# Gating into the final buffer, logits in groups of four, and a column-tiled second expert layer in a fused attention and two-expert-layer kernel

## The chip, the core and the metric

The kernel runs on one core of one Trainium2 chip. TensorE multiplies matrices into PSUM (eight banks of 128 x 512 words), VectorE, ScalarE and GpSimd work on tiles of 128 partitions, and SyncE issues the transfers (DMA). Every engine takes its instructions in the order of the program and waits for others by semaphores. The metric is the time of one execution in microseconds (us); shorter is better. Each verdict compares medians of several executions.

## What is computed

Three stages follow one another on 4608 tokens (8 batches of 576) of 512 features:

```python
# 1. linear attention, 8 heads of 64
q_s = softmax(q, axis=-1);  k_s = softmax(k, axis=2)
kv = einsum('bhsd,bhse->bhde', k_s, v)
x = einsum('bhsd,bhde->bhse', q_s, kv)         # tokens x 512
# 2. first expert layer: w_in 512 x 2048, w_out 2048 x 512
h = x @ w_in
g = h * cos(h)
x = g @ w_out
# 3. second expert layer: 8 experts of 4 slots, w1 512 x 1024, w2 1024 x 512 each
logits = x @ phi                                # 4608 x 32 slots
slot_input = softmax(logits, axis=0).T @ x      # 32 x 512
for e in range(8):
    slot_out[e] = relu(slot_input[e] @ w1[e]) @ w2[e]
out = softmax(logits, axis=1) @ slot_out
```

The kernel never forms `g @ w_out` for all tokens. It multiplies w_out by phi first (the 2048 x 32 matrix `w2sb`), so that logits come straight from g, and it sums g over the tokens with the slot weights before it multiplies by w_out.

## The kernel before

**Parts and tiles.** The tokens are cut into ten parts: parts 0 to 7 of 512 tokens, parts 8 and 9 of 256 (the last 512 tokens in halves). A part has 16 tiles, one for each 128 of the 2048 hidden features; `s = 16*d + f` counts them, and an even part from 2 on and part 8 start at another feature block (`tile_of`).

**A tile of the first expert layer.** `mm1` is 12 matmuls of 128 x 128 by 512 (256 in the halves), because x and w_in are each split into a high and a low word, into one of three PSUM banks `ps_h` (L700). `round_u` (L708 on ScalarE or L710 on VectorE, by the list `V_ACT`), `frac` (L714, VectorE), `sine` (L719) and `square` (L722, ScalarE) and `gate` (L725, VectorE) make g in one of four buffers `T`. `logits` (L736) then takes a pair of tiles: for each tile, one fp32 matmul for each 128 tokens, with the 32 columns of `w2sb` as weights, into 32-partition strips of one bank `ps_LT`: four strips in the wide parts, two in the halves. In the trace an fp32 matmul is two instructions. `g_tr` (L744, VectorE) writes g, transposed in blocks of 32 x 32, into `G`. `G` has 20 rows; a part uses 16 in four quarters, so that a part can begin one quarter of its own while the part before still holds its four. T is given back after logits and transposes.

**After each part.** `p1` copies the logits out, `p2` (L763, L768) spreads them by small matmuls to the partitions where they are needed, `p3` to `p5` make the running maximum and the slot weights, and `g_mm` (L828) multiplies weights and transposed g in 16 tiles of 32 x 32 of the array; `g_add` (L841) adds to the running sum `gacc` with a rescaling. A part's `g_mm` needs all 16 transposes, and the next part's later quarters of G need `g_mm`. For part 9 there is another form (L814): four times the instructions, a quarter of the output, added (L841, narrow) to a sum that `e_fold` has folded to a quarter before (L946, L952).

**The tail.** `e_tr` transposes the folded sum (L965), `e_si` multiplies it by w_out (L976), `e_siT` scales and turns it (L985 to L1000). `e_w1` (L1006) is the first matrix of the second expert layer, for two groups of four experts: weights of 32 columns, four column tiles, 64 instructions a group. `e_h` (L1018, L1020) and `e_hT` (L1028) make the hidden values; `e_w2` (L1040) multiplies by w2 in units of 1 MB, each in 16 tiles of 32 x 32 and four PSUM banks, one for each expert of the group; `e_so` (L1049, L1050) adds the four banks in pairs, `e_sx` (L1058, L1064) spreads the result, and `e_mm` (L1074) with `e_ev` (L1082) and `e_out` (L1085) write nine blocks of 1 MB. The weights, 36 units of 1 MB (`load_unit`, L920), go into buffers as these come free; `units_after` says which operation frees each. `keep_warm` (L1324) puts filler matmuls on TensorE before the first work (37) and in the tail (up to 100).

**The order.** A planner, `Issue`, holds every operation with a cost in us, its predecessors, a ring that it takes a buffer from (`m`: four PSUM banks, `h`: three, `T`: four) and a place. It plays the program through and gives each free engine the ready operation with the lowest place; the order that comes out is the program's order on each engine. Places of repeated operations are read from `PLACES`. The operations of a tile are in `step_ops`, those after a part in `post_ops`, those of the tail at the end. Here the transposes stand behind nearly everything (`TR`), and logits stand 1.6 tiles ahead; in part 0 (`TR0`) both stand ahead:

```python
op(("g", s), DVE, cost(0.06, 0.54), gate, s, at=s, give="h", after=[("sq", s)])
op(("tr", s), DVE, cost(0.08, 0.62), g_tr, s, at=s + tr_at[0], after=[("g", s)] + fresh)
```

`fresh` names the `g_mm` that held this quarter of G.

## Time and profile before

| | |
|---|---|
| median of three executions | 737.7 us (736.66 to 738.56) |
| the profiled execution | 738.9 us, of which the span of the trace is 737.0 us |
| TensorE matmuls busy | 687.9 us, 93% of the span |
| VectorE, ScalarE, GpSimd busy | 559.2, 449.8, 136.1 us |
| mean granted TensorE clock | 0.975 of full |
| transferred | 97.68 MB |

The trace is that of one execution. A row of a timeline gives the start in us from the span's start, the time that the row covers, the engine, the line of the program, the operation, output and input, the shape and how many instructions are merged in it; in brackets stands how long the engine was idle before and what ended that. `PEld` is TensorE loading weights, which overlaps with its matmuls. Matmuls overlap one another too, so the distance between starts says more than the length of a row. In a table by stretch each engine has its busy time and, after the x, its instructions; then come the granted TensorE clock, the share of time in which the 16 DMA engines were busy, and GB/s.

### The profile page before, as it was taken

How to read it: one execution, taken by the hardware profiler on the slowest of the kernel's cores; microseconds unless marked ns; L12 is line 12 of the kernel's file. 1: busy time of each engine (PE TensorE's matmuls, PEld its weight loads, DVE VectorE, ACT ScalarE, POOL GpSimd, SP SyncE). 2: the span in 40 equal slices, each digit the busy share in tenths (PEclk: the TensorE clock that was granted, in tenths of full speed). 3: DMA queues.
4: the chain of work that ended last, by engine and by line, in shares of the span. 5: the costliest groups of instructions: out<-in, count | busy, mean ns of one | idle time of the engine just before them, and what ended most of it. 6: DMA issues, size and time to landing. Idle time of an engine off the chain costs nothing.

```text
span 737.0 us, 17679 instructions
## 1 busy us (share of the span) xinstructions
PE 687.9 (93%) x7516; PEld 499.3 (68%) x7516; DVE 559.2 (76%) x1075; ACT 449.8 (61%) x758; POOL 136.1 (18%) x133
## 2 busy tenths in 40 slices
PE   7688999899999999999999999999999999889991
PEld 7465767677777766776777777677677787754450
DVE  6799999788898888798788887788776878611142
ACT  2669976956867756955947485584565557600041
POOL 3334522321411414114201250021010000000000
PEclk9899999999999999999999999999999999989996
DMA  9989960051241421320151103000030417989748
GB/s 275 335 326 239 330 199 2 1 142 46 60 100 30 117 43 29 81 62 18 30 130 30 29 15 131 2 29 1 2 103 18 163 31 247 374 299 406 309 163 353
DMA packets 69295, 97.68 MB, mean 133 GB/s; under 512 B 40416, under 2 KB 49632, under 8 KB 63968
## 3 DMA queue, kind: packets, MB, share of 16 engines
q1 hardware_dynamic: 69216, 96.55, 39.8%
q8 instruction: 59, 0.97, 0.6%
q14 instruction: 20, 0.16, 0.1%
HBM read 82.90 MB, written 13.63 MB: 131 GB/s over the span
## 4 chain that ended last, share of the span: by engine, by line
PE 70%; DVE 13%; ACT 9%; DMA 3%; issue 3%; POOL 0%; DVEq 0%; ACTq 0%; POOLq 0%
PE ps_h L700 42%; PE ps_m L828 5%; PE ps_LT L736 5%; PE ps_m L1040 2%; PE ps_m L354 2%; PE ps_LT L1324 2%; PE ps_m L493 2%; PE ps_m L395 2%; DVE T L714 2%; ACT T L719 2%; DVE T L725 2%; PE ps_h L1006 2%; ACT T L722 2%; DMA out_dram<-ob 1%; DMA KVB<-in_k_dram 1%
## 5 line engine op out<-in xcount | busy, mean ns | idle before, releaser
L700 PE MATMUL ps_h<-XH,W 128*128 128x512 f32 x1024 | 345.7, 405 | 0.5 <-DVE T L725 0.5
L700 PEld LDWEIGHTS ps_h<-XH,W 128*128 128x128 f32 x1024 | 193.6, 189 | 58.2 <-issue 12.9
L700 PE MATMUL ps_h<-XL,W 128*128 128x512 f32 x512 | 202.4, 395 | 0.7 <-DVE XL L418 0.7
L719 ACT ACTIVATE T<-T 128x512 f32<-128x512 f32 (+1 forms) x160 | 94.3, 589 | 110.9 <-DVE T L714 108.9
L725 DVE SCALAR_TENSOR_TENSOR T<-T,ps_h 128x512 f32<-128x512 f32 (+1 forms) x160 | 100.1, 627 | 46.0 <-ACT T L722 43.9
L700 PEld LDWEIGHTS ps_h<-XL,W 128*128 128x128 f32 x512 | 97.0, 189 | 19.7 <-DVE XL L418 1.2
L714 DVE SCALAR_TENSOR_TENSOR T<-T,ps_h 128x512 f32<-128x512 f32 (+1 forms) x160 | 100.2, 628 | 11.5 <-ACT T L708 9.2
L744 DVE STREAM_TRANSPOSE G<-T 128x512 f32<-128x512 f32 (+1 forms) x160 | 102.0, 648 | 1.6
L722 ACT ACTIVATE T<-T 128x512 f32<-128x512 f32 (+1 forms) x160 | 94.0, 588 | 4.3
L341 POOL TENSOR_TENSOR B<-Q,qm 128x512 f32<-128x512 f32 x34 | 36.4, 1088 | 207.0 <-PE ps_m L354 106.6
L708 ACT ACTIVATE T<-ps_h,magic 128x512 f32<-128x512 f32 (+1 forms) x84 | 53.2, 634 | 32.6 <-PE ps_h L700 32.4
L319 POOL TENSOR_TENSOR Q<-Q,qm 128x512 f32<-128x512 f32 x36 | 38.0, 1066 | 133.7 <-DVE qm L316 132.1
L736 PE MATMUL ps_LT<-T,wphi 128*32 128x128 f32 x1152 | 53.6, 281 | 4.1 <-DVE T L725 3.8
L710 DVE TENSOR_SCALAR T<-ps_h 128x512 f32<-128x512 f32 (+1 forms) x76 | 48.2, 634 | 10.8 <-PE ps_h L700 10.7
L736 PEld LDWEIGHTS ps_LT<-T,wphi 128*32 128x32 f32 x1152 | 29.2, 109 | 33.5 <-issue 18.5
L700 PE MATMUL ps_h<-xe,W 128*128 128x256 f32 x384 | 50.2, 286 | 0.0
L700 PEld LDWEIGHTS ps_h<-xe,W 128*128 128x128 f32 x384 | 46.9, 188 | 3.2 <-issue 3.2
L472 POOL TENSOR_TENSOR KVB<-KVB,km 128x576 f32<-128x576 f32 x28 | 39.2, 1434 | 31.6 <-ACT km L469 31.6
L828 PE MATMUL ps_m<-G,A 32*32 32x512 f32 x1088 | 38.9, 598 | 0.6 <-DVE A L795 0.5
L719 ACT ACT_TABLE_LOAD x29 | 37.2, 1283 | 0.5
L1324 PEld LDWEIGHTS ps_LT<-ones,ident 128*128 128x128 f32 x178 | 27.7, 242 | 10.6 <-issue 8.7
L1324 PE MATMUL ps_LT<-ones,ident 128*128 128x128 f32 x178 | 30.1, 334 | 4.2 <-issue 2.4
(167 smaller groups left out, 771.1 us busy)
## 6 DMA issues: line engine op xcount, KB each, us to landing
w_u<-in_moe_w_dram SPq DMA_DIRECT2D x22, 1024.0 KB, 8.0
KVB<-in_k_dram SPq DMA_DIRECT2D x16, 576.0 KB, 5.1
KVB<-in_v_dram SPq DMA_DIRECT2D x32, 288.0 KB, 6.1
out_dram<-ob SPq DMA_DIRECT2D x9, 1024.0 KB, 10.7
G<-in_moe_w_dram SPq DMA_DIRECT2D x8, 1024.0 KB, 8.4
rwi<-in_moe_w_in_dram SPq DMA_DIRECT2D x7, 1024.0 KB, 9.5
rwo<-in_moe_w_out_dram SPq DMA_DIRECT2D x5, 1024.0 KB, 7.7
wo<-G SPq DMA_DIRECT2D x16, 256.0 KB, 4.9
```

Of the source, the lines that this page charges most:

```text
L472: (nc.vector if dve else nc.gpsimd).tensor_tensor(out=k_t[:, t], in0=k_t[:, t], in1=km[:, t].unsqueeze(1).to_broadcast([128, KC, 64]), op= ...
L700: nc.tensor.matmul(out=u_t[s], lhsT=w[:, wi, kk, o:o + 128], rhs=x[xi][:, kk], start=(kk == 0 and n == 0), stop=(kk == 3 and n == 2),)
L708: nc.scalar.activation(out=t, in_=u_t[s], func=ACTF.Identity, bias=magic)
L710: nc.vector.tensor_scalar(out=t, in0=u_t[s], scalar1=MAGIC, scalar2=None, op0=ALU.add)
L714: nc.vector.scalar_tensor_tensor(out=t, in0=t, scalar=MAGIC, in1=u_t[s], op0=ALU.subtract, op1=ALU.subtract)
L719: nc.scalar.activation(out=t_t[s], in_=t_t[s], func=ACTF.Sin, scale=math.pi)
L722: nc.scalar.activation(out=t_t[s], in_=t_t[s], func=ACTF.Square, scale=math.sqrt(2.0))
L725: nc.vector.scalar_tensor_tensor(out=t_t[s], in0=t_t[s], scalar=1.0, in1=u_t.pop(s), op0=ALU.subtract, op1=ALU.mult)
L736: nc.tensor.matmul(out=lt_t[d][32 * c:32 * c + 32, 0:128], lhsT=w2sb[:, f], rhs=g[:, 128 * c:128 * c + 128], start=(i % NF == 0), stop=(i ...
L744: nc.vector.transpose(out=gs(d)[:, tile_of(d, i)], in_=t_t[s])
L828: nc.tensor.matmul(out=st["gp"][i][32 * c:32 * c + 32].rearrange("p (f b) -> p f b", f=NF), lhsT=ee[o, 32 * j:32 * j + 32], rhs=gs(d)[o, : ...
L1324: nc.tensor.matmul(out=warm[when][:, 0:128], lhsT=ident, rhs=ones, start=True, stop=True)
```

## The change

`gate` writes g straight into its place in `G`, T is given back there, and the transpose is done in place in G after the logits have read it. `logits` takes n tiles at once: in part 0 pairs as before, in parts 1 to 8 fours, in part 9 fours and, at the end, pairs (`NTL`). In the halves, four column tiles hold two tiles at a time, and `p2` sums the two strips. Part 9 uses the common form of `g_mm`; its sum goes to a buffer of its own (`g9`), is folded and is added to the earlier folded sum. `e_w2` uses 128 rows and four column tiles in place of 16 small tiles, into one PSUM bank, and starts after all of `e_w1`; `e_so` and `e_sx` handle the two halves of 256 columns on two engines. The filler is one matmul of 512 columns in fp32r in place of one of 128 in fp32. All places and the lists of who does what are new.

```diff
-    "TR": [352.1, -1.6],
-    "TR0": [-31.4, -260.3],
...
-    "V_ACT": [[2, 3, 5, 7, 9, 10, 11, 13, 15], [0, 1, 2, 4, 8, 10, 13, 14], [1, 5, 6, 8, 9, 11, 12, 14, 15]],
...
+    "TR": [350.5, -1.4],
+    "TR0": [235.9, -125.9],
...
+    "V_ACT": [[0, 4, 5, 8, 9, 10, 11, 12, 13, 14], [2, 3, 4, 5, 6, 7, 8, 9, 10, 11, 13, 14], [0, 3, 6, 7, 8, 10, 11, 14]],
...
+    "NTL": [[1, 3, 5, 7, 9, 11, 13, 15], [3, 7, 11, 15], [3, 7, 11, 13, 15]],
...
-    "TE": [-328.0, -346.1, -469.8, 431.3, -184.9, 140.8],
...
+    "TE": [-84.2, -443.3, -703.4, 431.4, -449.3, 370.8],
...
+    def g_of(s):
+        d, i = divmod(s, NF)
+        return gs(d)[:, tile_of(d, i)]
...
     def gate(s):
         nc.vector.scalar_tensor_tensor(
-            out=t_t[s], in0=t_t[s], scalar=1.0, in1=u_t.pop(s), op0=ALU.subtract, op1=ALU.mult
-        )
...
-    def logits(s):
+            out=g_of(s), in0=t_t.pop(s), scalar=1.0, in1=u_t.pop(s), op0=ALU.subtract,
+            op1=ALU.mult,
+        )
...
+    def logits(s, n):
...
         d = s // NF
-        if s % NF == 1:
+        if s % NF == n - 1:
             lt_t[d] = pst("LT", 1)
-        for i in (s - 1, s):
-            f, g = tile_of(d, i % NF), t_t[i]
-            for c in range(parts[d][2] // 128):
+        k = parts[d][2] // 128
+        m = 4 // k
+        for i in range(s - n + 1, s + 1):
+            f, g, f0 = tile_of(d, i % NF), g_of(i), i % NF
+            for c in range(k):
+                o = 32 * (c + k * (f0 % m))
                 nc.tensor.matmul(
-                    out=lt_t[d][32 * c:32 * c + 32, 0:128], lhsT=w2sb[:, f],
-                    rhs=g[:, 128 * c:128 * c + 128], start=(i % NF == 0), stop=(i % NF == NF - 1),
+                    out=lt_t[d][o:o + 32, 0:128], lhsT=w2sb[:, f],
+                    rhs=g[:, 128 * c:128 * c + 128], start=(f0 < m), stop=(f0 >= NF - m),
                 )
...
     def g_tr(s):
...
-        d, i = divmod(s, NF)
-        nc.vector.transpose(out=gs(d)[:, tile_of(d, i)], in_=t_t[s])
+        nc.vector.transpose(out=g_of(s), in_=g_of(s))
...
-        nc.scalar.copy(out=st["lt"][:r], in_=lt_t.pop(d)[:r, 0:128])
+        nc.scalar.copy(out=st["lt"], in_=lt_t.pop(d)[:, 0:128])
...
     def p2(d, part):
...
         pm = st["r" if part == 0 else "t"] = misc()
         if part == 0:
             for c in range(r // 32):
+                for n in range(c, 4, r // 32):
+                    nc.tensor.matmul(
+                        out=pm[:, 128 * c:128 * c + 128], lhsT=rc[:, n], rhs=st["lt"],
+                        start=(n == c), stop=(n + r // 32 >= 4),
+                    )
+        else:
+            for n in range(0, 128, r):
                 nc.tensor.matmul(
-                    out=pm[:, 128 * c:128 * c + 128], lhsT=rc[:r, c], rhs=st["lt"][:r],
-                    start=True, stop=True,
+                    out=pm[:, 0:r], lhsT=st["lt"], rhs=ident[:, n:n + r], start=(n == 0),
+                    stop=(n + r == 128),
                 )
-        else:
...
     def g_mm(d, jq):
...
-        if d == NB:
-            for j in range(4 * jq, 4 * jq + 4):
-                for i in range(4):
-                    o = slice(32 * i, 32 * i + 32)
-                    for n in range(4):
-                        nc.tensor.matmul(
...
-                            ),
-                            lhsT=ee[o, 32 * j:32 * j + 32],
-                            rhs=gs(d)[o, 4 * n:4 * n + 4, 32 * j:32 * j + 32],
-                            start=(j == 0), stop=(j == 7), tile_position=(32 * i, 32 * n),
-                        )
-            return
...
     def g_add(d, i):
-        nf = NF if d < NB else 4
-        gp = st["gp"][i][:, 0:32 * nf].rearrange("p (f b) -> p f b", f=nf)
-        dst = acc["g"][:, 0:nf, 32 * i:32 * i + 32]
-        if d == 0:
+        gp = st["gp"][i].rearrange("p (f b) -> p f b", f=NF)
+        dst = acc["g"][:, :, 32 * i:32 * i + 32]
+        if d == NB:
+            if i == 0:
+                acc["g9"] = sbt([128, NF, 128], "A", name="g9")
+            dst = acc["g9"][:, :, 32 * i:32 * i + 32]
+            (nc.vector.tensor_copy if i % 2 else nc.scalar.copy)(out=dst, in_=gp)
+        elif d == 0:
             nc.vector.tensor_copy(dst, gp)
         else:
             nc.vector.scalar_tensor_tensor(
...
     def e_fold(part):
...
+        old = acc["g"][:, 0:4].rearrange("p f b -> p (f b)")
+        if part % 2 == 0:
+            src = acc["g9" if part else "g"]
             tl_["fold"] = misc()
             for n in range(4):
...
                     out=tl_["fold"][32 * n:32 * n + 32], lhsT=r32,
-                    rhs=acc["g"][:, 4 * n:4 * n + 4].rearrange("p f b -> p (f b)"),
+                    rhs=src[:, 4 * n:4 * n + 4].rearrange("p f b -> p (f b)"),
...
                 )
+        elif part == 1:
+            nc.scalar.copy(out=old, in_=tl_.pop("fold"))
         else:
-            nc.scalar.copy(
-                out=acc["g"][:, 0:4].rearrange("p f b -> p (f b)"), in_=tl_.pop("fold")
+            nc.vector.scalar_tensor_tensor(
+                out=old, in0=old, scalar=ac, in1=tl_.pop("fold"), op0=ALU.mult, op1=ALU.add
             )
...
     def e_w2(eg, u):
...
-            so_t["p"] = [misc() for j in range(4)]
+            so_t["p"] = misc()
         for q4 in range(4):
-            for j in range(4):
-                o = slice(32 * j, 32 * j + 32)
-                nc.tensor.matmul(
-                    out=so_t["p"][j][32 * q4:32 * q4 + 32], lhsT=tl_["hT"][o, eg, 4 * u + q4],
-                    rhs=ut["w2", eg, u][o, q4], start=(eg == 0 and u == 0),
-                    stop=(eg == 1 and u == 7), tile_position=(32 * j, 32 * q4),
-                )
+            nc.tensor.matmul(
+                out=so_t["p"][32 * q4:32 * q4 + 32], lhsT=tl_["hT"][:, eg, 4 * u + q4],
+                rhs=ut["w2", eg, u][:, q4], start=(eg == 0 and u == 0),
+                stop=(eg == 1 and u == 7),
+            )
...
     def e_so(i):
...
-            so_t["s"] = sbt([128, 2, 512], "gacc", name="so_s")
-        nc.scalar.copy(out=so_t["s"][:, i], in_=so_t["p"][2 * i])
-        nc.vector.tensor_tensor(
-            out=so_t["s"][:, i], in0=so_t["p"][2 * i + 1], in1=so_t["s"][:, i], op=ALU.add
-        )
+            so_t["s"] = sbt([128, 512], "gacc", name="so_s")
+        o = slice(256 * i, 256 * i + 256)
+        (nc.vector.tensor_copy if i else nc.scalar.copy)(out=so_t["s"][:, o], in_=so_t["p"][:, o])
...
-                out=so_t["q"], lhsT=rr.rearrange("p r s -> p (r s)"), rhs=so_t["s"][:, part],
-                start=(part == 0), stop=(part == 1),
+                out=so_t["q"][i][:, 0:256], lhsT=rr.rearrange("p r s -> p (r s)"),
+                rhs=so_t["s"][:, o], start=True, stop=True,
...
-            so_t["b"] = sbt([128, 512], "wphi", name="so")
-            nc.scalar.copy(out=so_t["b"], in_=so_t["q"])
+            if i == 0:
+                so_t["b"] = sbt([128, 512], "wphi", name="so")
+            (nc.vector.tensor_copy if i else nc.scalar.copy)(
+                out=so_t["b"][:, o], in_=so_t["q"][i][:, 0:256]
+            )
...
-           s, act, at=s, take="T", after=[("mm1", s), past("tr", s - 4), past("tl", (s - 4) | 1)])
...
-        op(("g", s), DVE, cost(0.06, 0.54), gate, s, at=s, give="h", after=[("sq", s)])
-        op(("tr", s), DVE, cost(0.08, 0.62), g_tr, s, at=s + tr_at[0], after=[("g", s)] + fresh)
-        if f % 2:
-            op(("tl", s), PE, 0.5 if nt == 512 else 0.4, logits, s, at=s + tr_at[1],
-               after=[("g", s), ("g", s - 1), past("w2_ev", w // 2) if b == 0 else None,
-                      past("p1", d - 1) if f == 1 else None, past("tl", s - 2)]
-               + [past("warm", i) for i in range(NWARM)] * (s == 1))
-            op(("Tfree", s), PE, 0.0, nothing, at=s, give=("T", "T"),
-               after=[("tl", s), ("tr", s), ("tr", s - 1)])
...
+        op(("g", s), DVE, cost(0.06, 0.54), gate, s, at=s, give=("h", "T"), after=[("sq", s)] + fresh)
+        last = [t for t in tls(d) if t >= f][0]
+        if f == last:
+            n = f - max([t for t in tls(d) if t < f] + [-1])
+            op(("tl", s), PE, 0.15 + (0.215 if nt == 512 else 0.11) * n, logits, s, n, at=s + tr_at[1],
+               after=[("g", i) for i in range(s - n + 1, s + 1)]
+               + [past("w2_ev", tile_of(d, i) // 2) for i in range(f - n + 1, f + 1)] * (b == 0)
+               + [past("p1", d - 1) if f == n - 1 else past("tl", s - n)]
+               + [past("tl", i) for i in range(s - n - 3, s)]
+               + [past("warm", i) for i in range(NWARM)] * (d == 0 and f == n - 1))
+            for i in range(s - n + 1, s + 1):
+                op(("tr", i), DVE, cost(0.08, 0.62), g_tr, i, at=i + tr_at[0], after=[("tl", s)])
...
-            op(("g_mm", d, jq), PE, 1.08 if d < NB else 1.6, g_mm, d, jq, at=s0 + po[4], take=None if jq else "m",
+            op(("g_mm", d, jq), PE, 1.08, g_mm, d, jq, at=s0 + po[4], take=None if jq else "m",
...
-            op(("g_add", d, i), DVE, 0.67 if d < NB else 0.25, g_add, d, i, at=s0 + po[5], give="m",
+            on_act = d == NB and i % 2 == 0
+            op(("g_add", d, i), ACT if on_act else DVE, 0.58 if on_act else 0.67, g_add, d, i,
+               at=s0 + po[5], give="m",
...
+               + ([("w2_sum", 7)] if d == 0 else [("p5", d)] + [("g_add", d, 0)] * (i > 0) if d == NB else []))
...
-        nc.tensor.matmul(out=warm[when][:, 0:128], lhsT=ident, rhs=ones, start=True, stop=True)
+        nc.tensor.matmul(
+            out=warm[when], lhsT=ones_r, rhs=ones_r.unsqueeze(1).to_broadcast([128, 4, 128]),
+            start=True, stop=True,
+        )
...
+    op(("fold", 2), PE, 1.0, e_fold, 2, at=L + 24, take="m",
+       after=[("fold", 1)] + [("g_add", D, i) for i in range(4)])
+    op(("fold", 3), DVE, 0.7, e_fold, 3, at=L + 24, give="m", after=[("fold", 2)])
...
-        + [[end[7]], [("tl", L + 15), ("tr", L + 15), ("tr", L + 14)]]
...
+        + [[end[7]], [("g", L + 15)]]
+        + [[("g_mm", D, 1)]] * 2 + [[("fold", 2)]]
...
             op(("w2", eg, u), PE, 0.95, e_w2, eg, u, at=L + TE[4 + eg],
-               take=None if eg or u else "m", n_take=4,
-               after=[("hT", eg), past("w2", eg, u - 1) or past("w2", eg - 1, 7), *lus(("w2", eg, u))])
+               take=None if eg or u else "m",
+               after=[("hT", eg), ("w1", 1, 3, 1), past("w2", eg, u - 1) or past("w2", eg - 1, 7),
+                      *lus(("w2", eg, u))])
...
-        op(("so", i), DVE, 1.2, e_so, i, at=L + 17, give=("m", "m"),
+        eng, a, c = (DVE, 0.36, 0.36) if i else (ACT, 0.33, 0.33)
+        op(("so", i), eng, a, e_so, i, at=L + 17, give=() if i == 0 else "m",
...
-           after=[("sx", 2), ("c3", D), past("om", b - 1), past("oe", b - 2, 3)])
+           after=[("sx", 2), ("sx", 3), ("c3", D), past("om", b - 1), past("oe", b - 2, 3)])
```

## Rows read from the trace of the kernel before

**Rows 1.** The page, its busy line: busy us, share of the span and instructions of each engine.

```profile
PE 687.9 (93%) x7516; PEld 499.3 (68%) x7516; DVE 559.2 (76%) x1075; ACT 449.8 (61%) x758; POOL 136.1 (18%) x133
```

**Rows 2.** The table by stretch, us from the span's start. The stretches are part 5, part 9, the tail up to the last matmul of `e_si`, from there to the end of `e_w2`, and the output.

```profile
387.09:450.11 63.02, 62.59 (x658) 47.10 (x654) 53.08 (x96) 43.30 (x68) 16.89 (x15) 1.00 0.16 48
...
605.71:638.40 32.69, 32.55 (x329) 27.54 (x329) 26.16 (x70) 22.37 (x49) 0.00 (x0) 1.00 0.83 302
638.40:660.42 22.02, 16.28 (x339) 11.43 (x338) 5.90 (x22) 4.72 (x12) 0.00 (x0) 0.85 0.85 314
660.42:703.20 42.78, 41.02 (x703) 20.38 (x704) 6.46 (x6) 1.37 (x2) 0.00 (x0) 1.00 0.80 322
...
707.90:737.00 29.10, 12.04 (x289) 4.60 (x288) 11.42 (x18) 9.64 (x18) 0.00 (x0) 0.79 0.79 326
```

**Rows 3.** Timeline of TensorE's matmuls in part 5, around one pair of logits tiles, and a stretch of the main loop.

```profile
392.43 0.39 PE L700 MATMUL ps_h<-XH,W 128*128 128x512 f32 x1
392.75 0.64 PE L736 MATMUL ps_LT<-T,wphi 128*32 128x128 f32 x16
...
393.67 0.40 PE L700 MATMUL ps_h<-XL,W 128*128 128x512 f32 x1
...
402.33 0.39 PE L700 MATMUL ps_h<-XL,W 128*128 128x512 f32 x1
...
403.01 0.39 PE L700 MATMUL ps_h<-XL,W 128*128 128x512 f32 x1
```

**Rows 4.** Timeline of TensorE's matmuls behind `g_mm`, in part 2 (four logits tiles) and in part 6 (two); each group stands between the last matmul of `g_mm` and the next tile of the main loop.

```profile
209.31 1.08 PE L736 MATMUL ps_LT<-T,wphi 128*32 128x128 f32 x32
210.32 0.49 PE L700 MATMUL ps_h<-XH,W 128*128 128x512 f32 x1
...
471.88 0.64 PE L736 MATMUL ps_LT<-T,wphi 128*32 128x128 f32 x16
472.46 0.50 PE L700 MATMUL ps_h<-XH,W 128*128 128x512 f32 x1
```

**Rows 5.** Timeline of TensorE's matmuls in part 9.

```profile
626.58 4.58 PE L700 MATMUL ps_h<-xe,W 128*128 128x256 f32 x36
631.09 0.63 PE L736 MATMUL ps_LT<-T,wphi 128*32 128x128 f32 x8
631.65 3.14 PE L700 MATMUL ps_h<-xe,W 128*128 128x256 f32 x24
634.71 0.63 PE L736 MATMUL ps_LT<-T,wphi 128*32 128x128 f32 x8
```

**Rows 6.** Who waited for whom: in all, times, the longest (us). The two rows of logits that waited for a gate.

```profile
PEld ps_LT L736 <- DVE T L725: 8.1, 15, 1.5
...
PE ps_LT L736 <- DVE T L725: 3.8, 6, 1.2
```

**Rows 7.** Timeline of VectorE: the gate of the fifth tile of part 6, and the narrow additions of part 9.

```profile
476.48 0.69 DVE L725 SCALAR_TENSOR_TENSOR T<-T,ps_h 128x512 f32<-128x512 f32 x1 [1.36 <-ACT T L722]
...
649.81 1.12 DVE L841 SCALAR_TENSOR_TENSOR gacc<-gacc,ac,ps_m 128x128 f32<-128x128 f32 x4 [3.66 <-PE ps_m L814]
```

**Rows 8.** Timeline of TensorE's matmuls: `g_mm` of part 8 and the fold, then `p2`, `g_mm` of part 9, a group of fillers and the transposes of the tail.

```profile
615.38 2.35 PE L828 MATMUL ps_m<-G,A 32*32 32x512 f32 x64
617.66 0.63 PE L736 MATMUL ps_LT<-T,wphi 128*32 128x128 f32 x8
...
622.92 1.07 PE L946 MATMUL ps_m<-gacc,r 128*32 128x512 f32 x8
...
641.99 0.71 PE L763 MATMUL ps_m<-LTs,rc 64*128 64x128 f32 x4 [0.80 <-ACT LTs L755]
...
644.67 2.45 PE L814 MATMUL ps_m<-G,A 32*32 32x128 f32 x131
648.25 1.87 PE L814 MATMUL ps_m<-G,A 32*32 32x128 f32 x125 [1.13 <-issue]
...
653.07 1.86 PE L1324 MATMUL ps_LT<-ones,ident 128*128 128x128 f32 x7 [2.42 <-issue]
654.73 1.06 PE L965 MATMUL ps_m<-ident,gacc 128*128 128x128 f32 x4
```

**Rows 9.** The chain that ended last, in order of time (start, us, what): `e_w1` of group 0.

```profile
663.76 7.20 PE ps_h L1006 x64
```

**Rows 10.** Timeline of TensorE's matmuls at the end of `e_w2`: two units, fillers, `e_sx`, the first output block.

```profile
699.40 1.14 PE L1040 MATMUL ps_m<-G,hT 32*32 32x512 f32 x32
...
702.00 1.14 PE L1040 MATMUL ps_m<-G,hT 32*32 32x512 f32 x32
703.08 2.05 PE L1324 MATMUL ps_LT<-ones,ident 128*128 128x128 f32 x16
704.96 1.88 PE L1058 MATMUL ps_m<-so_s,rr 128*128 128x512 f32 x4
...
707.89 1.14 PE L1074 MATMUL ps_m<-so,cst 32*32 32x512 f32 x32
```

**Rows 11.** The table by stretch in the second expert layer, before and after the last load has landed.

```profile
684.80:695.50 10.70, 10.30 (x196) 5.76 (x196) 2.71 (x2) 0.69 (x1) 0.00 (x0) 1.00 0.97 402
695.50:703.20 7.70, 7.06 (x149) 3.40 (x138) 0.00 (x0) 0.00 (x0) 0.00 (x0) 1.00 0.03 9
```

**Rows 12.** The table by stretch, 2 us behind the row at 653.07 of rows 8.

```profile
654.00:656.00 2.00, 2.00 (x11) 2.00 (x10) 0.00 (x0) 0.17 (x1) 0.00 (x0) 0.50 0.97 336
```

65 lines of the change are left out of this document (32 added, 33 removed), and 10 rows, old and new, of the table PLACES.

## The prediction, made before the changed kernel was run

> **What bounds the kernel now.** I read the page first, then stretches of the program, then single instructions around the places that the change touches.
>
> The page's busy line [rows 1] names TensorE: 687.9 of 737.0 us, VectorE next with 559.2. The table by stretch [rows 2] says where that holds. In part 5 of the first expert layer TensorE is busy 62.59 of 63.02 us, VectorE 53.08, ScalarE 43.30: what TensorE issues there is the time. The same holds for the last half part (32.55 of 32.69 us), where the DMA share is 0.83 as well. After the last expert-layer tile (638.4) comes a chain with one thing at a time: up to 660.42 VectorE is busy only 5.90 us and TensorE 16.28 of 22.02, much of it filler. From 660.42 to 703.2 the two stages of the second expert layer run, TensorE 41.02 of 42.78 us, DMA share 0.80. From 707.9 the output is written, DMA share 0.79 of 29.1 us; nothing in the change touches its pace, so it only starts earlier or later.
>
> **Logits groups in parts 1 to 7.** A matmul of the main loop follows the one before by 0.227 us (402.33 to 403.01 is three) [rows 3]. Around a lone pair of logits tiles, 392.43 to 393.67 is 1.24 us where two steps would be 0.45: the detour costs 0.79. The pure work of a tile is seen where a group stands behind other small matmuls: four tiles take 1.01 us (209.31 to 210.32), two take 0.58 (471.88 to 472.46) [rows 4], so two tiles are 0.43 and the rest of the 0.79, 0.36 us, is entering and leaving. Groups of four in place of pairs take four groups out of each of the seven parts, 28 in all. If all stood alone: 28 x 0.36 = 10.1 us. If all stood beside other small work: two pairs cost 1.16, one four 1.01, so 28 x 0.15 = 4.2 us. The chain of a part has both kinds, and nothing favours one: I take 7.1 (bounds 4.2 and 10.1).
>
> **Packed columns in the last two half parts.** There a pair of 256-wide tiles keeps two of the four column tiles busy. From 626.58 to 631.09 36 matmuls and an exit take 4.51 us, from 631.65 to 634.71 24 take 3.06, so one is 0.121 us, and 24 of them with the 0.56 of the group and its edges (631.09 to 634.71, 3.62) leave 0.72 for a pair [rows 5]: as much as a pair of twice the width. Eight pairs a part cost 5.8 us. After, part 8 has four groups of four that fill the columns as a 512-wide pair does, 0.79 each, 3.2: a gain of 2.6. Part 9 has three of them and two of two (0.79 less half of 0.43, 0.58): 3.5, a gain of 2.3. Spreading the packed logits back takes two more small matmuls and one more transpose a part; two such take 0.71 in the tail (641.99) [rows 8], so +0.5 in part 8. Together -4.4.
>
> **G in place of T.** A T buffer is given back at the gate, not after logits and transpose. The transpose is the same instruction, now behind the logits group of four. TensorE waited for a gate ahead of logits 8.1 us at weight loads and 3.8 at matmuls, 21 times [rows 6]; 35 of 80 groups go. I count -2.5 (bounds 0 and -5). Some 24 roundings move from VectorE to ScalarE, which has the room [rows 2]. Places, the conversion stage and the warm-up: 0 (bounds -3 and +3), since part 0 keeps its pairs and its loads.
>
> The body: -7.1 - 4.4 - 2.5 = -14.0.
>
> **From the last tile to the expert input.** The wider spreading: +0.5. The last weighted sum goes from 644.67 to 649.81, 256 small instructions with a stall of 1.13 in which TensorE waited for nothing [rows 7, 8]; in the form of the other parts it has 64, which take 2.28 (615.38 to 617.66), twice that at the lower clock: I take 3.2, -1.9 (bounds -2.8 and -0.5). Four narrow adds, 1.12 us together, become four wide copies on two engines, 2 x 0.69 by the wide gate [rows 7]: +0.3. A second fold is new in the chain: 1.07 for its matmuls (622.92), 0.69 for the add, 0.2 for two hand-offs, +2.0. Then between the end of the adds (650.93) and the transposes (654.73) the trace loses 3.8 us to fillers and a stall of 2.42 [rows 8]. It was not waiting for data; a shorter instruction stream should meet less of it, but the new program has fillers too: half, -1.9 (bounds -3.6 and 0). Sum -1.0 (bounds -3.6 and +2.3).
>
> **Second expert layer.** Today its first stage is split by its second: w2 of group 0 runs ahead of most of w1 of group 1, and the last two loads wait for w1 of group 1. The DMA share is 0.97 up to 695.5 and 0.03 after [rows 11], and the last w2 units run at 699.40 and 702.00, with fillers between, ending at 703.08 [rows 10]. After the change all of w1 comes first. A unit in four column tiles is 8 instructions, 0.90 us by the same shape in w1 (7.20 for 64) [rows 9], against 1.07. TensorE's own work from 663.76 is then 14.4 + 16 x 0.90 = 28.8, so 692.6, and the loads set the end: 695.5, 0.5 for landing, 0.9 for a unit, 696.9. That is -6.2; fillers laid ahead of a unit that has landed keep 1.2 of it: -5.0 (bounds -7 and 0).
>
> **Output of the experts.** From 703.08 to 707.89 [rows 10] two copies and two adds run in turn, two wide matmuls (1.88) and a copy. After: a half copy, two half matmuls, a half copy. A half copy is between 0.35 and 0.69 (half and whole of [rows 7]), I take 0.45; the matmuls 0.94; hand-offs 0.3: 2.1, so -2.7, less 0.4 for fillers: -2.3 (bounds -2.8 and -1.0). By the Trainium skill (PSUM — Partial Sum Buffer, PSUM bank collisions raise a hardware error), two engines may not touch one bank and quadrant at a time, so the two half copies of one bank would have to run in turn; by that the estimate is 2.5 in place of 2.1. No run here shows it.
>
> The tail: -1.0 - 5.0 - 2.3 = -8.3.
>
> **The sum.** -14.0 - 8.3 = -22.3 on the profiled execution of 738.9 us (span 737.0 and 1.9 around it): 716.6. The median of the runs shown is 737.7, 1.2 below it, so 715.4.
>
> **Rivals.**
> A, the forecast, 715.4: both halves pay. Chance 0.55.
> B, the body pays, the w2 order does not: fillers and stalls stand where the waits stood, as at 653.07 [rows 8] and 702.00 [rows 10]. Against it: the loads end 7.6 us before the last unit. Then 737.7 - 14.0 - 1.0 - 2.3 = 720.4. Chance 0.18.
> C, TensorE starves while it waits for data in w2. With w1 done early each unit of 0.9 us waits for a load of about 2.6 (34 us for 13 units by the DMA share of that stretch), and TensorE may fall to its lower clock, as it stood at 0.50 of full, 1.2 GHz, at 654 to 656 after idling 2.42 us [rows 8, 12]. The last unit, the half matmuls and the first output block would take twice as long, 0.9 + 0.9 + 1.0: 718.2. Fillers speak against it. Chance 0.12. The Trainium skill (TensorE: Matmul & The Clock Gate, HAM oscillation — how this bites in real kernels) tells of just this: a burst of matmuls shorter than the wait for its load starts at the lower clock each time. The trace at 654 agrees with it.
> D, only the tail pays: the saved detours come back as idle time, because the order of the other engines sets the pace. For it: VectorE is at 84% in part 5. Against it: TensorE at 99%. 737.7 - 8.3 = 729.4. Chance 0.08.
> E, slower: the gate now writes into G, so it, and not the transpose, waits for the weighted sum of the part before. In part 6 that sum's matmuls leave the queue at 471.88 and the gate of the fifth tile starts at 476.48 [rows 4, 7]: 4.6 us in hand. The sum comes later by 0.43 (two more tiles in the last group) and by two more transposes behind it, 1.4: 2.8 us remain. If it came later by more than the 4.6, gate, ps_h and main loop would stop; a stop of 4 us in each of seven parts is 28 us, which outweighs all gains: 737.7 - 22.3 + 28 = 743.4. It decides from 3.2 us a part. Chance 0.05.
> F, no change, since the program's order absorbs it: 737.7, chance 0.02.
>
> **How the numbers follow.** The predicted time is A's. The smallest gain is 4.2 + 4.4 + 0 in the body and -2.3 + 0 + 1.0 in the tail, 7.3 us: 730; with 3 lost at the places 733. The largest is 10.1 + 4.4 + 5 and 3.6 + 7 + 2.8, 32.9: 705; with 3 won at the places 702. All ends at once are unlikely, so 702 to 731 holds A to D with little left out, E and F outside. Faster by over 0.3%, about what a measurement of this kernel can tell from no change (2.2 us): A to D less a little, 0.92; slower 0.05; within 0.03.
>
> **What would show each step.** Parts 1 to 7 shorter by 1 us each, with logits groups of 32 instructions; half parts 8 and 9 shorter by 2 us each; the stretch from the last tile to the expert input about as long as now; w2 after all of w1, ending some 1.5 us behind the last load; 2 to 2.5 us from there to the first output block; the output as long as now. The prediction is wrong if gates of fifth tiles stand waiting while TensorE idles, if part 0 moves by more than 3 us, or if fillers stand ahead of w2 units that have landed.

## The result, and the profile of the changed kernel

The changed kernel takes 719.4 us (median of runs from 719.15 to 721.51) against 737.9 for the kernel before, timed beside it: ratio 0.9758, 95% interval 0.9735 to 0.978. The forecast was 715.4 with a range of 702 to 731. The profiled execution took 721.5 us, the longest of the four; its span is 719.7 us, 17.3 less than before, where the forecast had 22.3 less. Start times of the main loop's parts and of the tail's steps, read from the two timelines, give this account (us):

| stretch | before | after | change | forecast |
|---|---|---|---|---|
| start to the first main-loop matmul | 32.06 | 38.97 | +6.9 | 0, bounds 3, for this row and the next |
| part 0 | 88.38 | 84.48 | -3.9 | |
| parts 1 to 7 | 450.03 | 440.72 | -9.3 | -7.1 - 2.5 |
| part 8 | 35.24 | 33.55 | -1.7 | -2.1 |
| part 9 | 32.62 | 31.86 | -0.8 | -2.3 |
| last main-loop matmul to the end of `e_si` | 22.06 | 20.57 | -1.5 | -1.0 |
| from there to the end of `e_w2` | 42.75 | 37.97 | -4.8 | -5.0 |
| from there to the first output block | 4.75 | 2.49 | -2.3 | -2.3 |
| output | 29.1 | 29.1 | 0 | 0 |

The busy line of the page (us, share of the span, instructions) beside [rows 1]: TensorE has 16 us less to do and VectorE 14.

```profile
PE 671.6 (93%) x6878; PEld 488.8 (68%) x6878; DVE 545.5 (76%) x1054; ACT 458.8 (64%) x773; POOL 140.2 (19%) x135
```

The table by stretch for parts 5 and 9 and the sum over parts 1 to 9 (columns as in [rows 2]: length, then busy time and count of TensorE, weight loads, VectorE, ScalarE, GpSimd, granted clock, DMA share, GB/s):

```profile
385.85:447.27 61.42, 59.95 (x634) 45.89 (x631) 46.96 (x84) 44.88 (x71) 11.26 (x10) 1.00 0.13 44
...
597.72:629.58 31.86, 31.55 (x342) 27.20 (x340) 24.67 (x70) 23.47 (x52) 0.00 (x0) 1.00 0.83 303
sum 506.13, PE 499.83 PEld 386.22 DVE 413.52 ACT 358.35 POOL 89.53; mean PE 55.54 PEld 42.91 DVE 45.95 ACT 39.82 POOL 9.95
```

The same sum for the kernel before:

```profile
sum 517.90, PE 511.40 PEld 383.85 DVE 428.44 ACT 347.71 POOL 91.97; mean PE 56.82 PEld 42.65 DVE 47.60 ACT 38.63 POOL 10.22
```

This is the main reading. Parts 1 to 9 lost 11.8 us, and TensorE's busy time in them lost 11.6; its idle time is 6.3 us, 6.5 before. The gain is work and edges (the entering and leaving of a group) that TensorE no longer has, and not waits that ended. Each of the two traces has one short fall of the granted clock in these parts, right behind a wait of TensorE: 0.76 over 131 to 138 us before, behind a wait of 1.90, and 0.57 over 376 to 380 us now, behind a wait of 2.85 for a maximum of K.

Timeline of TensorE: four logits tiles behind `g_mm` in part 7, and a packed group of four in part 8 (they answer to [rows 4] and [rows 5]); 1.01 us and 0.57 us from start to the next row:

```profile
530.64 1.08 PE L752 MATMUL ps_LT<-G,wphi 128*32 128x128 f32 x32
531.65 0.50 PE L708 MATMUL ps_h<-XH,W 128*128 128x512 f32 x1
...
580.86 0.64 PE L752 MATMUL ps_LT<-G,wphi 128*32 128x128 f32 x16
581.43 6.02 PE L708 MATMUL ps_h<-xe,W 128*128 128x256 f32 x48
```

Who waited for whom (us in all, times, longest): TensorE's main loop and logits for a gate, and gates for the weighted sum.

```profile
PE ps_h L708 <- DVE G L733: 2.7, 3, 1.4
PE ps_LT L752 <- DVE G L733: 2.3, 3, 0.9
...
DVE G L733 <- PE ps_m L830: 4.9, 5, 2.5
```

The head, on VectorE and TensorE. The tile of ones is now made from the identity, and on VectorE it stands behind the first maxima of K, which wait for a load; sixteen fillers that need it stand ahead of `k_tr`:

```profile
8.70 0.22 DVE L239 TENSOR_SCALAR ones<-ident 128x128 fp32r<-128x128 f32 x1
```
```profile
8.97 6.51 PE L1345 MATMUL ps_LT<-ones 128*128 128x512 f32 x16 [8.97 <-DVE ones L239]
15.31 0.38 PE L446 MATMUL ps_m<-ident,km 128*128 128x128 f32 x2
```

The tail, TensorE's timeline (answers to [rows 8] and [rows 10]):

```profile
633.19 2.08 PE L778 MATMUL ps_m<-LTs,rc 128*128 128x128 f32 x8 [0.80 <-ACT LTs L769]
...
637.76 3.03 PE L830 MATMUL ps_m<-G,A 32*32 32x512 f32 x64
640.71 2.56 PE L1345 MATMUL ps_LT<-ones 128*128 128x512 f32 x10
643.20 1.07 PE L957 MATMUL ps_m<-g,r 128*32 128x512 f32 x8
...
679.40 1.07 PE L1051 MATMUL ps_m<-w_u,hT 128*32 128x512 f32 x8 [0.62 <-DMA w_u<-in_moe_w_dram]
...
681.88 1.06 PE L1051 MATMUL ps_m<-w_u,hT 128*32 128x512 f32 x8 [0.52 <-DMA w_u<-in_moe_w_dram]
682.88 1.66 PE L1345 MATMUL ps_LT<-ones 128*128 128x512 f32 x6
684.47 1.06 PE L1051 MATMUL ps_m<-G,hT 128*32 128x512 f32 x8
685.46 1.66 PE L1345 MATMUL ps_LT<-ones 128*128 128x512 f32 x6
687.05 1.06 PE L1051 MATMUL ps_m<-G,hT 128*32 128x512 f32 x8
```

The thirteenth and fourteenth unit of `e_w2` wait for their loads; the last two stand behind six fillers each and start 0.13 and 0.25 us after their loads have landed (684.34 and 686.80). The last load lands 57.2 us behind the last main-loop matmul, 58.8 in the kernel before; the end of `e_w2` follows it by 1.3 us, by 6.0 before. No wait at a matmul is put down to "issue" in this trace.

### The profile page after: what moved, and what is told of

It reads as the page before. It is cut to its first block, busy times and chain, and to the rows that moved or that the text cites. A ratio compares the mean times of both kernels' runs of the same rounds, so it can differ in the third digit from the quotient of the medians.

```text
span 719.7 us, 16462 instructions
## 1 busy us (share of the span) xinstructions
PE 671.6 (93%) x6878; PEld 488.8 (68%) x6878; DVE 545.5 (76%) x1054; ACT 458.8 (64%) x773; POOL 140.2 (19%) x135
## 4 chain that ended last, share of the span: by engine, by line
PE 74%; DVE 9%; DMA 6%; ACT 5%; issue 3%; POOL 1%; SPq 1%; DVEq 0%; ACTq 0%; POOLq 0%
PE ps_h L708 49%; PE ps_m L830 6%; PE ps_LT L752 4%; PE ps_m L497 3%; DMA w_u<-in_moe_w_dram 2%; PE ps_m L399 2%; PE ps_m L358 2%; PE ps_LT L1345 2%; DMA out_dram<-ob 1%; DMA Q<-in_q_dram 1%; PE ps_m L778 1%; PE ps_h L1019 1%; DVE T L722 1%; DMA KVB<-in_k_dram 1%; PE ps_m L634 1%
## 5 line engine op out<-in xcount | busy, mean ns | idle before, releaser
L708 PE MATMUL ps_h<-XH,W 128*128 128x512 f32 x1024 | 340.2, 402 | 2.7 <-DVE G L733 2.7
L708 PEld LDWEIGHTS ps_h<-XH,W 128*128 128x128 f32 x1024 | 193.2, 189 | 56.7 <-issue 9.9
L733 DVE SCALAR_TENSOR_TENSOR G<-T,ps_h 128x512 f32<-128x512 f32 (+1 forms) x160 | 100.2, 629 | 56.4 <-ACT T L730 48.7
L722 DVE SCALAR_TENSOR_TENSOR T<-T,ps_h 128x512 f32<-128x512 f32 (+1 forms) x160 | 99.7, 628 | 14.8 <-ACT T L716 12.6
L759 DVE STREAM_TRANSPOSE G<-G 128x512 f32<-128x512 f32 (+1 forms) x160 | 95.5, 633 | 0.2 <-PE ps_LT L752 0.2
L716 ACT ACTIVATE T<-ps_h,magic 128x512 f32<-128x512 f32 (+1 forms) x106 | 68.6, 649 | 35.5 <-PE ps_h L708 34.5
L752 PE MATMUL ps_LT<-G,wphi 128*32 128x128 f32 x1152 | 41.9, 278 | 2.6 <-DVE G L733 2.3
L752 PEld LDWEIGHTS ps_LT<-G,wphi 128*32 128x32 f32 x1152 | 28.7, 109 | 17.2 <-issue 11.2
L718 DVE TENSOR_SCALAR T<-ps_h 128x512 f32<-128x512 f32 (+1 forms) x54 | 32.6, 606 | 7.8 <-PE ps_h L708 7.2
L1345 PE MATMUL ps_LT<-ones 128*128 128x512 f32 x86 | 27.3, 459 | 9.0 <-DVE ones L239 9.0
L1345 PEld LDWEIGHTS ps_LT<-ones 128*128 128x128 f32 x86 | 17.6, 218 | 19.3 <-DVE ones L239 9.0
```

The source lines that it names most:

```text
L708: nc.tensor.matmul(out=u_t[s], lhsT=w[:, wi, kk, o:o + 128], rhs=x[xi][:, kk], start=(kk == 0 and n == 0), stop=(kk == 3 and n == 2),)
L716: nc.scalar.activation(out=t, in_=u_t[s], func=ACTF.Identity, bias=magic)
L722: nc.vector.scalar_tensor_tensor(out=t, in0=t, scalar=MAGIC, in1=u_t[s], op0=ALU.subtract, op1=ALU.subtract)
L733: nc.vector.scalar_tensor_tensor(out=g_of(s), in0=t_t.pop(s), scalar=1.0, in1=u_t.pop(s), op0=ALU.subtract, op1=ALU.mult,)
L752: nc.tensor.matmul(out=lt_t[d][o:o + 32, 0:128], lhsT=w2sb[:, f], rhs=g[:, 128 * c:128 * c + 128], start=(f0 < m), stop=(f0 >= NF - m),)
L759: nc.vector.transpose(out=g_of(s), in_=g_of(s))
```

## The experiments

Part lengths repeat well from run to run where the order of the instructions is the same (part 7 took 57.29 to 57.41 us in eight of the kernels here), so edits of one part are read from lengths, and whole times as ratios to the kernel before. Part 4 is the exception: it took 69.5 to 70.2 us where it has the fall of the clock, and 67.33 in the run with `w2` free, where K's maximum is waited for 1.35 us and the clock stays at 1.00.

**The tile of ones made early.**

```
-    nc.vector.tensor_scalar(out=ones_r, in0=ident, scalar1=0.0, scalar2=1.0, ...)
+    nc.vector.memset(ones_f, 1.0)
+    nc.vector.tensor_copy(ones_r, ones_f)
```

> The changed kernel with one edit: the tile of ones for the filler matmuls comes from a memset and a copy at the start of VectorE's queue, no longer from the identity behind the first maxima of K. Theory (late ones hold the head): fillers start near 2 us, not at 8.97, the transposes of K's maxima come near 8.4, not 15.3, the first matmul of the first expert layer near 32, not 38.97; part 1 starts 3 to 7 us earlier than 123.45 and the time is 712.5 to 716.5. Rival (part 0 is paced by loads and conversions of the weights, so an early start is given back by its end): part 1 starts within 1 us of 123.45, time 718.4 to 720.

Measured: 714.5 us, ratio 0.9671 (0.9641 to 0.970). TensorE's timeline:

```profile
1.54 6.81 PE L1345 MATMUL ps_LT<-ones 128*128 128x512 f32 x16 [1.54 <-DVE ones L241]
8.19 0.41 PE L446 MATMUL ps_m<-ident,km 128*128 128x128 f32 x2
...
33.44 0.78 PE L708 MATMUL ps_h<-XH,W 128*128 128x512 f32 x1
```

`k_tr` comes 7.1 us earlier, the first main-loop matmul 5.5, part 1 at 117.03 and not 123.45. Part 0 takes 83.6 us, 84.5 in the changed kernel, so nothing was given back: the late ones held the head, and this version is faster than both kernels. The first main-loop matmul still comes 1.4 us later than in the kernel before, which no run explains.

**Logits in pairs everywhere.** The edit: `"NTL": [[1, 3, 5, 7, 9, 11, 13, 15]] * 3`.

> The changed kernel with logits in pairs again in all parts (packed columns and G in place kept). Theory (detours of TensorE): 28 more groups in parts 1 to 7 cost 4.2 to 10.1 us, 7.1 at the middle; in the half parts 7 more groups cost some 0.3 each, 2; the time is 719.4 + 9 = 728.5 (725.5 to 731.5). Rival (the other engines' order sets the pace, the saved detours are idle time): within 2 us of 719.4.

Measured: 744.9 us, ratio 1.0077 (1.0051 to 1.0103); by the ratios some 24 us more than the changed kernel, not 9. The table by stretch, part 6 and the sum over parts 1 to 9:

```profile
448.02:530.98 82.96, 71.77 (x683) 52.85 (x682) 48.19 (x88) 46.45 (x72) 11.83 (x10) 0.92 0.13 43
...
sum 530.24, PE 516.43 PEld 386.93 DVE 412.94 ACT 368.16 POOL 88.77; mean PE 57.38 PEld 42.99 DVE 45.88 ACT 40.91 POOL 9.86
```

TensorE is busy 16.6 us longer and idle 7.5 longer. Part 6 alone grew by 23.4. There the order comes apart, probably because the places were left as they were: TensorE waits 4.2 us for the attention's `KVB` and 3.9 for gates, and one gate stands behind the weighted sum as rival E had it:

```profile
DVE G L733 <- PE ps_m L830: 4.5, 1, 4.5
```

About 6.6 us of the busy time is the lower clock of part 6 (0.08 of 82.96, an estimate); the other 10 are the size of the detours. One edit of the groups over all parts thus mixes two things, and the next run takes them apart.

**Pairs in part 7 alone.** The edit: part 7 uses the first list of `NTL`, all others stay.

> The changed kernel with logits in pairs in part 7 alone; the instructions up to part 7 stand as in the changed kernel. Theory (a detour of TensorE costs its edges): four more groups in part 7, so it is longer by 0.6 (4 x 0.15, beside other small work) to 1.4 (4 x 0.36, alone), about 1.3 by the isolated groups (2 x 0.775 less 1.207 for each four); part 7 takes 58.0 to 58.8, not 57.39, the total 720 to 721. Rival (pairs or fours, the other engines set the pace): part 7 stays within 0.3 of 57.39.

Measured: 721.7 us, ratio 0.9754 (0.972 to 0.9789). Part 7 and part 8:

```profile
507.08:566.43 59.35, 59.35 (x502) 43.24 (x500) 44.33 (x79) 33.52 (x60) 2.05 (x2) 1.00 0.12 36
566.43:599.28 32.85, 32.21 (x398) 28.11 (x395) 27.98 (x72) 19.43 (x45) 0.00 (x0) 1.00 0.28 98
```

Part 7 takes 59.35 us, more than the 58.8 that was expected at most. It is 1.96 us longer and part 8 0.70 shorter, since a pair of tiles that fell behind the border now falls ahead of it (502 matmul records in part 7, 485 in the changed kernel): 1.27 for four more groups, 0.32 each. Over 28 groups that is 8.9 us, and parts 1 to 7 gained 9.3. That a group has a price, and its size, is shown in this one part; the whole time can't tell 1.3 us.

**Two column tiles in the half parts.** The edit: `o = 32 * c` with the old `start` and `stop`, and the old `p1` and `p2`; groups as changed.

> The changed kernel with the logits of the two half parts in two column tiles again (the groups of four stay). Theory by the small matmuls' number (one for 128 columns of one tile, packed or not): the groups cost the same, 0.77, and only the spreading after them shrinks, so part 8 is 33.0 to 33.6 and the stretch behind the last tile shorter by 0.5 to 1.3. Rival, the forecast's (packing fills the column tiles and halves the cost of a group): each group of four takes 1.2, not 0.77, part 8 is 35.2, part 9 33.3, the total 722.

Measured: 721.4 us, ratio 0.9749 (0.9714 to 0.9784). The same group of part 8 as above, and its follower:

```profile
579.84 1.07 PE L752 MATMUL ps_LT<-G,wphi 128*32 128x128 f32 x16
580.84 6.02 PE L708 MATMUL ps_h<-xe,W 128*128 128x256 f32 x48
```

1.00 us against 0.57 for the same 16 matmuls: filling the four column tiles nearly doubles their pace, and the theory by number is wrong. Part 8 is 1.2 us longer, part 9 0.9. But behind the last tile `p2` now takes 0.77 us and not 2.82, of which 1.27 is the lower clock that the changed kernel's trace has there (`p2` takes 1.55 in the run with `w2` free, at 1.00). From the start of part 7 to the end of `e_w2` it is 181.38 us against 181.33. The packing gains 2.0 in the parts and next to nothing in all; as the clock behind the last tile differs between these two traces (last section), some tenths of a microsecond stay open.

**The second stage of the second expert layer free again.** The edit: `("w1", 1, 3, 1)` taken out of what `w2` comes after.

> The changed kernel with the second stage of the second expert layer free to run ahead of the first stage's second half, as before. Theory (the order paid, since the last two loads wait for the first stage): the last load lands about 5 us later, and the time is 719.4 + 4.8 = 724.2 (722 to 726). Rival (the gain of 4.8 us in this stretch came from the four column tiles, 0.86 a unit and not 1.07, and from fewer fillers): the time stays at 719 to 721.

Measured: 719.6 us, ratio 0.9739 (0.9712 to 0.9767): no loss. In this trace the expert input came 2.1 us earlier by the clock (last section), so it is set against the run with pairs in part 7, which had that clock too: `e_w2` ends 59.08 us behind the last main-loop matmul against 58.03, and the last load lands at 58.0 against 56.7. The order is worth 1.05 us here, not 5.

**The old form of that stage in the new order.** The edit: `e_w2`, `e_so`, `e_sx` of the kernel before.

> The changed kernel with the second stage of the second expert layer in sixteen small tiles a unit, its sum over four banks and its two whole matmuls, as before, but behind all of the first stage, as changed. Theory (the last loads set the end, and what follows them counts): the two last units 0.4, copies, adds and matmuls 2.3; 722.1 (721.5 to 723.0). Rival (TensorE's own work in the stage sets the end): sixteen units at 1.07, not 0.86, 3.4 more; with the 2.3, 725.

Measured: 728.3 us, ratio 0.9838 (0.9802 to 0.9873). By the same yardstick `e_w2` ends at 63.14, not 58.03, and from there to the first output block it takes 4.86, not 2.51: 5.1 + 2.35, the rival's 3.4 and 1.7 more. Of the 5.1 us, 1.4 are a last load that lands later; the rest is that the end of `e_w2` follows this load by 5.0 us and not 1.3. TensorE stops twice where it waits for nothing that the trace shows (timeline; the second fence is the DMA queues from 675 to 678: packets, MB, share of 16 engines):

```profile
677.77 0.72 PE L1053 MATMUL ps_m<-G,hT 32*32 32x512 f32 x15 [1.31 <-issue]
...
683.97 1.15 PE L1053 MATMUL ps_m<-w_u,hT 32*32 32x512 f32 x30 [1.73 <-issue]
```
```profile
q1 hardware_dynamic: 169, 1.25, 99.6%
q8 instruction: 1, 0.02, 2.2%
```

**The order alone, in the kernel before.** The edit: `("w1", 1, 3, 1)` put into what `w2` comes after.

> The kernel before with the order alone: the second stage of the second expert layer waits for all of the first. Theory of the forecast (the order is the gain): the last two loads are issued about 11 us earlier, the second stage ends 5 us earlier, 737.7 - 5 = 732.7. Theory after the runs so far (the column tiles are the gain, the order is worth 1): 736.7 (735.5 to 738); sixteen units at 1.07 and the stalls between them stand behind the loads.

Measured: 741.0 us, ratio 1.0027 (0.9998 to 1.0055): no gain. The last load is issued 12.5 us earlier by the last main-loop matmul and lands 2.3 earlier, 56.5 us behind it and not 58.8 (first fence: DMA share of two stretches). The units don't follow (second fence), and `e_w2` ends 6.9 us behind the last load, 6.0 in the kernel before:

```profile
692.00:694.00 2.00, 2.00 (x55) 0.85 (x41) 0.00 (x0) 0.00 (x0) 0.00 (x0) 1.00 0.64 258
694.00:696.00 2.00, 2.00 (x41) 1.16 (x26) 0.00 (x0) 0.00 (x0) 0.00 (x0) 1.00 0.08 33
```
```profile
690.28 3.21 PE L1040 MATMUL ps_m<-w_u,hT 32*32 32x512 f32 x73 [1.76 <-issue]
...
700.12 1.60 PE L1324 MATMUL ps_LT<-ones,ident 128*128 128x128 f32 x12
701.65 1.14 PE L1040 MATMUL ps_m<-G,hT 32*32 32x512 f32 x32
```

TensorE comes late out of such stalls, and then the fillers, laid out for loads that come every 2.5 us, still stand between units that landed 5.4 to 5.8 us before. So the timeline has it; the old form without fillers was not run. With both runs the gain of this stretch belongs to the column tiles.

**No fillers behind the last tile.** The edit: `"NFILL": 0`.

> The changed kernel without any filler matmuls after the last tile. Theory (fillers stand ahead of work that is ready): 0.6 ahead of the weighted sum, 1.0 ahead of the second fold, 2 ahead of the last two units come back; 719.4 - 3.6 = 715.8 (715 to 718). Rival C of the forecast (TensorE starves and its clock falls): a granted clock of 0.50 in the last w2 units and the first output block, 719.4 + 3 = 722 or more.

Measured: 724.7 us, ratio 0.9784 (0.9741 to 0.9827), so the expected gain of 3.6 us is not there. By the whole times a loss is unclear, as the interval overlaps that of the changed kernel; in the traces `e_w2` ends 63.8 us behind the last main-loop matmul and not 58.5. Two stretches, and the last four units:

```profile
645.00:655.00 10.00, 7.60 (x40) 2.10 (x36) 1.49 (x2) 0.59 (x1) 0.00 (x0) 0.59 0.58 245
...
688.00:694.00 6.00, 3.00 (x16) 0.36 (x16) 0.00 (x0) 0.25 (x1) 0.00 (x0) 0.73 0.27 113
```
```profile
684.32 1.06 PE L1051 MATMUL ps_m<-w_u,hT 128*32 128x512 f32 x8 [1.32 <-DMA w_u<-in_moe_w_dram]
686.81 1.06 PE L1051 MATMUL ps_m<-w_u,hT 128*32 128x512 f32 x8 [1.42 <-DMA w_u<-in_moe_w_dram]
689.30 1.06 PE L1051 MATMUL ps_m<-G,hT 128*32 128x512 f32 x8 [1.43 <-DMA G<-in_moe_w_dram]
691.75 1.93 PE L1051 MATMUL ps_m<-G,hT 128*32 128x512 f32 x8 [1.39 <-DMA G<-in_moe_w_dram]
```

Rival C's mechanism is real once the fillers are gone: at a granted clock of 0.59 `e_si` takes 6.28 us and not 3.64. Of the four units that wait for loads three still take 1.06 us; the last takes 1.93. The units come every 2.49 us, as their loads land; with fillers they come every 2.58. The fillers cost a tenth of a microsecond a unit there, not one.

**The last two loads left out.** The edit: the units `("w2", 1, 6)` and `("w2", 1, 7)` read two buffers that are there.

> The changed kernel without its last two loads of expert weights: the last two units read two units that are there already, so the second layer's output leaves two units' weights out. Instructions and fillers stand as they did. Theory (the stream of loads sets the end of this stage): the second stage ends 2 x 2.6 us earlier, less what fillers keep, 3 to 5; 715.5 (714 to 716.5). Rival (TensorE's own stream and its fillers set the end): within 1 us of 719.4.

Measured: 719.9 us, ratio 0.9756 (0.9725 to 0.9788): no gain. The last three units:

```profile
679.85 1.07 PE L1054 MATMUL ps_m<-w_u,hT 128*32 128x512 f32 x8 [0.51 <-DMA w_u<-in_moe_w_dram]
...
682.43 1.06 PE L1054 MATMUL ps_m<-G,hT 128*32 128x512 f32 x8
...
685.01 1.06 PE L1054 MATMUL ps_m<-G,hT 128*32 128x512 f32 x8
```

They still come every 2.58 us. Loads set the time up to the fourteenth unit, and from there the fillers reproduce the pace of loads, present or not. Neither theory alone is right: taking away one of two limits that lie on each other shows nothing.

**Fewer fillers and early ones.** The edit: that of the first run, and 0.32 for 0.22 as a filler's cost.

> The changed kernel with the early tile of ones of the first experiment and fillers reckoned at 0.32 us and not 0.22 in the order's making, so that a third fewer stand ahead of the second fold and one fewer ahead of each late unit. Theory: the 6.4 us of the early ones, and 0.5 to 1.5 from fewer fillers; 712 (711 to 713.5). Rival (the loads set the end there, fillers stand in time that is lost anyway): as the early ones alone, 713 to 714.5.

Measured: 715.2 us, ratio 0.9683 (0.9643 to 0.9724), as the early ones alone. The expert input came 1.0 us earlier, and a unit waited longer for its load:

```profile
676.47 1.07 PE L1051 MATMUL ps_m<-w_u,hT 128*32 128x512 f32 x8 [0.75 <-DMA w_u<-in_moe_w_dram]
```

**Places.** Two runs cross the two structures with each other's places: the changed kernel with the `PLACES` of before (and its own `NTL`), and the kernel before with the new ones.

> The changed kernel with the places of the kernel before, and only the groups of the logits as changed. Theory (structure pays, places 0 with bounds of 3): 716.5 to 722.5. Rival (places and structure belong together: with the old places the gates that write into G wait for the weighted sum, TensorE stands still): 724 or more, with more than 5 us of gates waiting for the weighted sum.

> The kernel before with the places and the division of work between engines of the changed kernel. Theory (places fit one structure only, as the changed kernel with the old ones showed): slower than the kernel before by 5 to 40 us, in stops of TensorE in single parts. Rival (the new places are better in themselves and make up part of the gain): 725 to 735.

Measured: 757.8 us, ratio 1.0267 (1.0225 to 1.0309), and 776.0, ratio 1.0513 (1.0468 to 1.0557). In the first, TensorE waits 10.2 us for gates at main-loop matmuls (2.7 in the changed kernel) and part 1 takes 85.2 us; VectorE's additions wait for the weighted sum:

```profile
DVE gacc L847 <- PE ps_m L830: 15.2, 6, 5.0
```

In the second, part 6 takes 94.4 us. Neither set is better in itself; each fits the structure that it was made for.

## Why the prediction came out as it did

**The logits groups: right.** 0.32 us a group as measured by itself, between the two bounds of 0.15 and 0.36; 8.9 for 28 groups, forecast 7.1. That the parts gained just 9.3 is closer than single parts bear out, since other work moves between them: part 1 is 4.8 us shorter than before and part 4 3.6 longer.

**G in place of T: wrong, 0 and not -2.5.** This is read from sums, with the places changed as well. TensorE's idle time in parts 1 to 9 is as it was, and 2.85 of the 6.3 us that are left is the wait for K's maximum. Logits wait less for gates at their matmuls (3.8 us in [rows 6], 2.3 now), but the main loop waits 2.7 at its own, where the trace before has 0.5. A wait moved from one place to another. Rival E's mechanism is there too, 4.9 us of gates behind the weighted sum, 2.5 the longest, less than the 3.2 a part from which it was to decide; the longest falls in part 7, where TensorE is not idle at all. In the run with pairs everywhere it reaches 4.5 in the part that grows by 23 us. Giving T back late was not tried by itself, since groups of four need it early.

**Packed columns: the pace right, the sum wrong.** That packing takes nearly half off a group is shown. But part 8 and 9 together gained 2.5 us, not 4.4: TensorE's idle time in them rose from 0.7 to 1.3 us, and the rest is not settled. Behind the last tile the wider spreading cost 0.8 at the full clock (1.55 against 0.77) and 1.5 at the lower one (2.82 against 1.33 in the kernel before with new places), where the forecast had 0.5. Up to the end of `e_w2` next to nothing is left of it, since the loads reach the same time anyway: the last one lands 180.04 us behind the start of part 7 without the packing and 180.02 with it.

**The head: a term that was set to 0.** The forecast said that part 0 keeps its loads, and did not ask in which order VectorE would come to the new tile of ones. The start lost 7 us up to the first main-loop matmul and 3.0 up to part 1, the whole bound, and the experiment gives more than that back. Of the 4.9 us between the forecast for the profiled execution (716.6) and its 721.5 this is 3.0; another 1.5 is part 9. The forecast's own sign of error, part 0 moving by more than 3 us, showed it. Why part 0 itself became 3.9 us shorter no run shows.

**Last tile to expert input: -1.5 for -1.0.** The pieces: `g_mm` 3.03 (3.2 forecast), copies 1.3, the second fold with its add 1.9 (2.0 forecast), ten fillers that hold the fold back by 1.1 us behind the copies. The stall of 2.42 [rows 8] is gone. But this stall was no fixed property of the kernel before. The run with the order alone has the same instructions there, stops 1.05 us at the same place, and reaches the expert input 19.07 us behind the last main-loop matmul and not 22.06:

```profile
652.66 1.05 PE L1324 MATMUL ps_LT<-ones,ident 128*128 128x128 f32 x7 [1.05 <-issue]
```

The changed kernel needs 18.47 to 20.57 us for this stretch, by its clock (last section). So the size of this term is not settled, and that -1.5 lies near -1.0 is in part chance.

**Second expert layer: the size right, the cause wrong.** -4.8 measured for -5.0, but the forecast gave it to the order. The order alone is worth nothing in the kernel before and 1 us in the changed one. That the loads set the end after the change was right: the last unit ends 1.3 us behind the last load, 1.5 forecast. What failed is the reason for the 6 us by which the kernel before ends behind its last load (it lands at 697.1 us; the forecast took 696.0 from the DMA share). At 1.07 a unit the forecast's own sum for TensorE, 14.4 + 16 x 1.07, ends before the loads too, so the order alone should have closed this distance; in the run with the order alone it was 6.9. The sum left out the stalls in streams of small matmuls, of which the trace of before shows one of 1.13 us [rows 8], and it let units of the old form start as their loads land, which an order with fillers fixed ahead does not once TensorE is late. Fillers ahead of a landed unit cost 0.25 us at the last one, where it allowed 1.2. With the small tiles TensorE comes late and stays late; with the column tiles it is early and waits for loads.

**`e_so` and `e_sx`: right.** -2.26 for -2.3; the old form costs 2.35 more by itself. The two copies of the one bank do run in turn (0.37 and 0.42), as the rule of the Trainium skill has it (PSUM — Partial Sum Buffer, PSUM bank collisions raise a hardware error); the kernel's order asks for that as well, so the rule itself was not tested.

**Rivals.** B (720.4) lies nearest to the time, but by chance: the w2 stretch paid what A said. C did not happen at the units: the granted clock stayed at 1.00 there, and the run without fillers shows why. The trace of that run agrees only in part with the rule that the prediction named for it (Trainium skill, TensorE: Matmul & The Clock Gate, HAM oscillation — how this bites in real kernels): with units of 1 us every 2.49, the lower clock came at the fourth of them and not at each. D is refuted by the idle sums, 6.5 and 6.3. So the total lies in the range by a right reading of the logits groups and of the first output block, and by luck in the tail, where a right size stood for a wrong cause.

## What to carry to other kernels

Where an engine is busy without a gap, count what leaves its own stream: instruction groups and the edges around them, by a group measured alone; here this gave 8.9 us for the 28 groups, where the parts lost 9.3. Treat every new source of an early operand as a part of the change: ask at which place of its engine's queue it stands and which waits stand ahead of it, fillers included. And in an order written out ahead, fillers that stand for waits stay when the wait goes, so removing a limit shows nothing until the fillers go with it.
